# Moving batch 1's first scores, sums and values later in the stream of FFN matmuls

## The chip, the cores and the metric

One core of one Trainium2 chip. The metric is the device time of one execution in microseconds (us); medians of several runs are quoted. Engines: PE is TensorE, DVE is VectorE, ACT is ScalarE, POOL issues the loads, SP issues transposes and stores.

## The reference, cut to what matters

```python
k_proj = einsum('ks,bhsd->bhkd', E, k)            # 8 batches, 8 heads, seq 1024, head_dim 64, 64 projected keys
v_proj = einsum('ks,bhsd->bhkd', F, v)
attn = softmax(q @ k_proj.T / sqrt(64))           # per batch and head
x = (attn @ v_proj) ... reshaped to (8192, 512)
h = maximum(maximum(x @ w1, x @ w2), x @ w3)      # d_ff 768
out = h @ w_out                                   # float32
```

## The kernel before

PE works through 8 batches of two halves ("visits" `(b, ch)`). A visit has 6 FFN steps `up` (12 matmuls of 128x512 each: three weights, four contraction tiles) and 4 output steps `down` (6 matmuls each). The attention of the next batch is cut into small pieces, which a hand-made plan puts behind the steps. Here is the plan of batch 0, and the pieces it names:

```python
def scores(b, g, lo, nsi):        # needs qT and kpT; g is a pair of heads
    t, ns = two()                 # two PSUM banks out of 8
    ... 4 matmuls ...
def sc(b, g, lo=0, nsi=SI):       # scores; its exponential (ACT) is issued "later", in the next step
    ...
def za(b, g, ...):                # sums and values, then ln and exp on ACT, then the scaling on DVE
    z = sums(b, g, lo, nsi)       # needs the exponential
    av = values(b, g, lo, nsi)    # needs the projected values too
    invert(b, g, lo, nsi, z)      # ACT: zl = ln(z); zi = exp(-zl)
    scale_x(b, g, lo, nsi, av)    # DVE: xT = av * zi, which the FFN of batch b reads
def vproj(b): ...                 # 16 matmuls, needs v of batch b in SBUF
def qd(b, parts=1): ...           # DVE copies of q, then a DMA transpose per part -> qT

def up(b, ch, jt):
    ...
    early = jt == 0               # first step of a visit: the last contraction tile at the end,
    for i in range(3):            # so 9 matmuls run before xT of the last pair is needed
        h.append(bank())
        up_mm(h[i][0], i, b, ch, jt, range(NCT - early))
    ...                           # [cut] then h1s copy (ACT), two maxima (DVE)

# plan(0); a key is (half, step), steps 6 to 9 are output steps
(0, 7): [qd(1, 2), za(0, 2, *c1)],
...
(1, 0): [kproj(1)],
(1, 1): [kt(1)],
(1, 2): [sc(1, 0), sc(1, 1), vproj(1), ld(2)],
(1, 3): [za(1, 0), sc(1, 2)],
(1, 4): [za(1, 1), sc(1, 3)],
(1, 5): [za(1, 2)],
(1, 7): [za(1, 3)],
```

The copies of an output step go from PSUM to SBUF on ACT (`down(..., "s")`), except in the very first visit. Banks are dealt by a small clock model in the program, so moving a piece can deal all later banks anew.

The softmax here doesn't subtract the row's maximum and nothing guards it: scores larger than these inputs give would overflow.

Of the kernel before, what the change touches and what calls it, by code (L numbers as in the profile page):

```python
# [15 lines left out]
def kernel(  # L16
# [62 lines left out]
    def bank():  # L79
        n = min(range(8), key=lambda n: free[n])  # L80
        deal((n,))
        return psum_t[:, n, :], (n,)
# [110 lines left out]
    def scores(b, g, lo, nsi):  # L193
        t, ns = two()
        n = nsi // 2
        for c in range(2):
            for hp in range(2):
                rows = slice(hp * HALF, (hp + 1) * HALF)
                at = g * SI + lo + c * n
                nc.tensor.matmul(  # L200
                    out=t[c * HALF:(c + 1) * HALF, hp, 0:n * P],
                    lhsT=kpTs[b][rows, g, :],
                    rhs=qTs[b][rows, at:at + n, :],
                    start=True, stop=True,
                )
        return t[:, :, 0:n * P], ns, pe(n * MM / 4 + 0.1)

    def exps(b, g, lo, nsi, sc):
        t, ns, ready = sc
        pTs[b, g, lo] = att.tile([P, 2, CHUNK], BF16, name="pT", bufs=4)[:, :, 0:nsi * HALF]  # L210
        nc.scalar.activation(out=pTs[b, g, lo], in_=t, func=AF.Exp, scale=scale)  # L211
        runs("s", ready, 0.17 + nsi * 0.107, ns)
# [14 lines left out]
    def sums(b, g, lo, nsi):  # L227
        return pair_mm(b, g, lo, nsi, lambda rows, hp: ones[rows])

    def invert(b, g, lo, nsi, z):  # L230
        t, ns, ready = z
        zl = att.tile([P, 2, CHUNK], FP32, name="zl", bufs=1)[:, :, 0:nsi * HALF]
        nc.scalar.activation(out=zl, in_=t, func=AF.Ln)  # L233
        runs("s", ready, 0.17 + nsi * 0.107, ns)
        if nsi == SI:
            zi = att.tile([P, 2, CHUNK], FP32, name="zi", bufs=2)
        else:
            zi = att.tile([P, 2, CHUNK // 2], FP32, name="zi0", bufs=4)
        nc.scalar.activation(out=zi, in_=zl, func=AF.Exp, scale=-1.0)  # L239
        zis[b, g, lo] = zi, runs("s", ready, 0.17 + nsi * 0.107)  # L240

    def values(b, g, lo, nsi):
        if b not in xTs:
            xTs[b] = att.tile([P, NCT, SI, P], BF16, name="xT")
        return pair_mm(b, g, lo, nsi, lambda rows, hp: vps[b][rows, 2 * g + hp, :])

    def scale_x(b, g, lo, nsi, av):
        t, ns, ready = av
        zi, when = zis.pop((b, g, lo))
        nc.vector.tensor_tensor(  # L250
            out=xTs[b][:, g, lo:lo + nsi, :].rearrange("a (c s) p -> a c (s p)", c=2),
            in0=t, in1=zi, op=ALU.mult,
        )
        runs("v", max(ready, when), 0.17 + nsi * 0.13, ns)
# [8 lines left out]
    def sc(b, g, lo=0, nsi=SI):  # L263
        def f():
            t = scores(b, g, lo, nsi)
            later.append(lambda: exps(b, g, lo, nsi, t))
        return f

    def za(b, g, lo=0, nsi=SI, then=False):
        def f():  # L270
            z = sums(b, g, lo, nsi)
            av = values(b, g, lo, nsi)
            invert(b, g, lo, nsi, z)
            if then:
                later.append(lambda: scale_x(b, g, lo, nsi, av))
            else:
                scale_x(b, g, lo, nsi, av)
        return f
# [84 lines left out]
    def vproj(b):  # L363
        def f():
            t, ns = bank()
            proj(b, 2, t, (LO, HI), 4 * D)

            vps[b] = att.tile([P, H, D], BF16, name="vp")
            for hh, hs in enumerate((LO, HI)):
                i = t[hh * HALF:(hh + 1) * HALF, 0:4 * D].rearrange("a (h d) -> a h d", d=D)  # L370
                for to in range(2):
                    copy("sv"[hh], vps[b][to * HALF:(to + 1) * HALF, hs, :], i, ns, 0.4)
        return f
# [161 lines left out]
                most(hs[:, jt] if i == 1 else hTs[0, 0][:, jt, :], *h[jt], hs[:, jt])  # L535
                then((i, jt))

    def up(b, ch, jt):
        if jt == 0:
            hTs[b, ch] = ffn_sb.tile([P, NJT, CHUNK], BF16, name="hT")  # L540
        h, done = [], []
        early = jt == 0
        for i in range(3):
            h.append(bank())
            up_mm(h[i][0], i, b, ch, jt, range(NCT - early))
            done.append(clock["pe"])
        if early:
            for i in range(3):
                up_mm(h[i][0], i, b, ch, jt, (NCT - 1,))
                done[i] = clock["pe"]  # L550
        h1s = ffn_sb.tile([P, CHUNK], FP32, name="h1s")
        nc.scalar.copy(out=h1s, in_=h[0][0])  # L552
        r = runs("s", done[0], 0.6, h[0][1])
        run_later()
        m12 = ffn_sb.tile([P, CHUNK], FP32, name="m12")
        nc.vector.tensor_tensor(out=m12, in0=h[1][0], in1=h1s, op=ALU.max)  # L556
        runs("v", max(r, done[1]), 0.69, h[1][1])
        most(hTs[b, ch][:, jt, :], *h[2], m12)
# [50 lines left out]
    def ld(b):  # L609
        return lambda: load(b)  # L610

    def plan(b):
        n = b + 1
        if b == 0:
            c1 = (SPC, SPC)
            return {
                (0, 6): [za(0, 1, *c1), sc(0, 3, *c1)],
                (0, 7): [qd(1, 2), za(0, 2, *c1)],
                (0, 8): [za(0, 3, *c1)],
                (1, 0): [kproj(1)],  # L620
                (1, 1): [kt(1)],
                (1, 2): [sc(1, 0), sc(1, 1), vproj(1), ld(2)],
                (1, 3): [za(1, 0), sc(1, 2)],
                (1, 4): [za(1, 1), sc(1, 3)],
                (1, 5): [za(1, 2)],
                (1, 7): [za(1, 3)],
            }
        if b == 1:
            return {
                (0, 1): [qd(2)],  # L630
                (0, 5): [kproj(2), vproj(2), ld(3)],
                (0, 6): [kt(2)],
                (0, 7): [sc(2, 0)],
                (0, 9): [za(2, 0), sc(2, 1)],
                (1, 1): [za(2, 1), sc(2, 2)],
                (1, 3): [za(2, 2), sc(2, 3)],
                (1, 5): [za(2, 3)],
                (1, 6): [qd(3)],
            }
        if b == 2:  # L640
            return {
                (0, 2): [kproj(3), vproj(3), ld(4)],
                (0, 3): [kt(3)],
                (0, 4): [sc(3, 0)],
                (0, 6): [za(3, 0), sc(3, 1)],
                (1, 0): [za(3, 1), sc(3, 2), qd(4)],
                (1, 2): [za(3, 2), sc(3, 3), kproj(4), vproj(4), ld(5)],
                (1, 4): [kt(4)],
                (1, 5): [za(3, 3), sc(4, 0)],
            }  # L650
        if n == B:
            return {}
        out = {
            (0, 1): [za(n, 0), sc(n, 1)],
            (0, 3): [za(n, 1), sc(n, 2)],
            (0, 9): [za(n, 2), sc(n, 3)],
            (1, 3): [za(n, 3)],
        }
        if n + 1 < B:
            out[0, 6] = [qd(n + 1)]  # L660
            out[0, 9] += [kproj(n + 1), vproj(n + 1)]
            out[1, 1] = [kt(n + 1)]
            out[1, 3] += [sc(n + 1, 0)]
        if n + 2 < B:
            out[1, 1] += [ld(n + 2)]
        return out

    for b in range(B):
        p = plan(b)

        def behind(ch, step):
            for f in p.get((ch, step), []):
                f()

        for ch in range(NCHUNK):
            if (b, ch) == (0, 0):
                c1 = (SPC, SPC)
                up_first({
                    (0, 0, 5): [lambda: v_pair(2)],
                    (0, 1, 2): [lambda: x(2)],  # L680
                    (0, 1, 5): [lambda: v_pair(3), ld(1)],
                    (0, 2, 2): [lambda: x(3)],
                    (2, "a", 2): [qp(0, (0, 1), *c1)],
                    (2, "a", 4): [qp(0, (2, 3), *c1)],
                    (2, 0): [sc(0, 0, *c1)],
                    (2, 2): [sc(0, 1, *c1)],
                    (2, 4): [za(0, 0, *c1, then=True), sc(0, 2, *c1)],
                })
                run_later()
                behind(0, NJT - 1)  # L690
            else:
                for step in range(NJT):
                    up(b, ch, step)
                    behind(ch, step)
            for tt in range(SPC):
                down(b, ch, tt, "v" if (b, ch) == (0, 0) else "s")
                behind(ch, NJT + tt)
# [30 lines left out]
```

## Time and profile before

| | |
|---|---|
| time | 406.68 us median of 3 runs (406.23 to 407.16) |
| PE busy | 391.0 of 405.1 us |
| longest PE wait inside the run | 1.80 us, for qT of batch 1 |
| from the first scores (57.41) to the next visit's first h1s copy (78.43) | 21.02 us |

The page of the kernel before, its lines on PE, the granted clock by slice, the DMA engines by slice, and the chain that ended last. The digits are tenths in 40 slices of 10.1 us.

```profile
PE 391.0 (97%) x2330; PEld 178.2 (44%) x2374; DVE 199.9 (49%) x309; ACT 190.9 (47%) x278; POOL 31.6 (8%) x44
...
PEclk9999999999999999999999999999999999999999
DMA  9999999949927994991898119950510202020202
...
PE 83%; DMA 10%; ACT 2%; issue 1%; POOL 1%; DVE 1%; ACTq 0%; POOLq 0%
```

PE is the bound, at full clock. But in the first eight slices (81 us) the DMA engines are busy 90% or more, and the chain gives DMA 10% of the span: up to 57 us the loads of weights and of q lead it.

The timeline of PE where batch 1's attention begins (start us, duration us, engine, line, operation, out<-in, count, and in brackets the idle time just before and what ended it; a trace can lack a few matmul records, so a count of x11 stands for 12). L496 are FFN matmuls, L200 scores, L284 projections, L220 sums and values, L591 output steps:

```profile
52.86 2.75 PE L496 MATMUL banks<-xT,w_sb 128*128 128x512 bf16 x12
57.41 0.63 PE L200 MATMUL banks<-qT,kpT 64*64 64x512 bf16 x8 [1.80 <-DMA qT<-q_p]
57.97 1.06 PE L284 MATMUL banks<-v_t,efT 128*64 128x256 bf16 x16
58.97 2.76 PE L496 MATMUL banks<-xT,w_sb 128*128 128x512 bf16 x11
61.66 0.41 PE L220 MATMUL banks<-pT,ones 64*64 64x512 bf16 x4
```

and the first line of ACT's timeline after 78 us, the next visit's first h1s copy:

```profile
78.43 0.58 ACT L552 COPY h1s<-banks 128x512 f32<-128x512 f32 x1 [1.57 <-PE banks L496]
```

PE ends FFN step 2 at 55.61 (52.86 + 2.75), and stands until 57.41 for the transposed queries. Then scores, value projection, and step 3 follow.

When the two loads came: first the load of v of batch 1, then the transpose of the first half of q. Each fence has the issue and the time from issue to landing:

```profile
L189 POOL DMA_DIRECT2D v_t<-in_v_dram x1: 873/873/873, 25.8 to 25.8; - x1
...
DMA to landing us min/median/max: 30.4/30.4/30.4
```

```profile
L331 SPq DMA_TRANSPOSE qT<-q_p x1: 8108/8108/8108, 44.6 to 44.6; - x1
...
DMA to landing us min/median/max: 12.8/12.8/12.8
```

v landed at 25.8 + 30.4 = 56.2, qT at 44.6 + 12.8 = 57.4. Both are later than PE wants them (55.61).

### The profile page before, as it was taken

To read this page: it belongs to the slowest core of one execution; us is meant where nothing else is said; L and a number is where in the kernel's file an instruction comes from. 1 tells how busy PE (TensorE), PEld (TensorE's weight loads), DVE (VectorE), ACT (ScalarE), POOL (GpSimd) and SP (SyncE) were. 2 spreads that over 40 slices of the span, in tenths; PEclk is the share of its full clock that TensorE was granted. 3 is DMA by queue.
4 is the path that set the end of the run, shared out by engine and by line. 5 is a ranking of instruction groups with operands and counts; after the bars stand their busy time and mean duration, and the time that the engine had idled before them with its cause. 6 is when DMAs were issued, how large, how long until landed. Compare 5 with 4: busy or idle time off the path is not lost.

```text
span 405.1 us, 5869 instructions
## 1 busy us (share of the span) xinstructions
PE 391.0 (97%) x2330; PEld 178.2 (44%) x2374; DVE 199.9 (49%) x309; ACT 190.9 (47%) x278; POOL 31.6 (8%) x44
## 2 busy tenths in 40 slices
PE   6899989999999999999999999999999999999996
PEld 3444433444444535444544445444544444444443
DVE  2348746462655527537353655626464363525251
ACT  2612429624763366555544555437535556432322
POOL 7440011002000100200200002000000000000000
PEclk9999999999999999999999999999999999999999
DMA  9999999949927994991898119950510202020202
GB/s 148 206 205 207 230 200 166 242 114 126 256 34 210 177 237 106 146 246 25 213 187 181 44 37 236 205 148 2 141 69 1 104 2 104 2 104 0 105 0 104
DMA packets 62667, 53.33 MB, mean 132 GB/s; under 512 B 30128, under 2 KB 58288, under 8 KB 62640
## 3 DMA queue, kind: packets, MB, share of 16 engines
q0 software_dynamic: 28512, 28.31, 44.0%
q1 hardware_dynamic: 33984, 24.51, 19.7%
q8 instruction: 18, 0.29, 0.3%
q10 hardware_dynamic: 144, 0.13, 0.1%
q14 instruction: 9, 0.07, 0.1%
HBM read 57.15 MB, written 16.78 MB: 183 GB/s over the span
## 4 chain that ended last, share of the span: by engine, by line
PE 83%; DMA 10%; ACT 2%; issue 1%; POOL 1%; DVE 1%; ACTq 0%; POOLq 0%
PE banks L496 55%; PE banks L591 19%; PE banks L220 4%; DMA q_t<-in_q_dram 3%; DMA qT<-q_p 3%; DMA w_sb<-in_moe_w_dram 3%; PE banks L284 3%; PE banks L200 2%; ACT pT L211 1%; ACT zl L233 1%; DVE xT L250 1%; ACT zi L239 1%; DMA out_dram<-o_sb 0%; POOL k_t L147 0%; POOL q_t L152 0%
## 5 line engine op out<-in xcount | busy, mean ns | idle before, releaser
L496 PE MATMUL banks<-xT,w_sb 128*128 128x512 bf16 x1118 | 254.7, 379 | 2.8 <-issue 0.6
L496 PEld LDWEIGHTS <-w_sb 128*128 128x128 bf16 x1152 | 109.5, 98 | 136.8 <-issue 9.8
L556 DVE TENSOR_TENSOR m<-banks,h1s 128x512 f32<-128x512 f32 x90 | 62.0, 689 | 85.1 <-ACT h1s L552 53.8
L552 ACT COPY h1s<-banks 128x512 f32<-128x512 f32 x90 | 52.4, 582 | 89.9 <-PE banks L496 87.2
L591 PE MATMUL banks<-wout_sb,hT 128*128 128x512 bf16 x370 | 84.8, 379 | 0.7 <-issue 0.3
L250 DVE TENSOR_TENSOR xT<-banks,zi 128x1024 bf16<-128x1024 f32 (+1 forms) x36 | 39.8, 1106 | 75.8 <-ACT zi L239 56.4
L506 DVE TENSOR_TENSOR hT<-banks,m 128x512 bf16<-128x512 f32 x90 | 62.3, 692 | 10.1 <-DVE m L556 0.5
L99 ACT COPY o_sb<-banks 128x512 f32<-128x512 f32 (+1 forms) x60 | 34.8, 580 | 53.0 <-PE banks L591 52.9
L591 PEld LDWEIGHTS <-hT 128*128 128x128 bf16 x378 | 36.0, 98 | 45.4 <-DVE hT L506 2.8
L233 ACT ACTIVATE zl<-banks 128x1024 f32<-128x1024 f32 (+1 forms) x36 | 33.5, 930 | 29.8 <-PE banks L220 28.9
L211 ACT ACTIVATE pT<-banks 128x1024 bf16<-128x1024 f32 (+1 forms) x36 | 33.2, 931 | 14.4 <-PE banks L200 14.4
L239 ACT ACTIVATE zi<-zl 128x1024 f32<-128x1024 f32 (+1 forms) x36 | 34.6, 962 | 1.1
L189 POOL DMA_DIRECT2D q_t<-in_q_dram x7 | 6.1, 878 | 204.1 <-DMA qT<-q_p 141.7
L200 PE MATMUL banks<-qT,kpT 64*64 64x512 bf16 (+1 forms) x144 | 13.7, 358 | 2.2 <-DMA qT<-q_p 1.8
L284 PEld LDWEIGHTS <-efT 128*64 128x64 bf16 x256 | 12.8, 110 | 5.0 <-issue 4.6
L220 PE MATMUL banks<-pT,ones 64*64 64x512 bf16 (+1 forms) x144 | 13.9, 376 | 0.8 <-DVE xT L250 0.3
L220 PE MATMUL banks<-pT,vp 64*64 64x512 bf16 (+1 forms) x144 | 13.3, 356 | 0.1
L99 DVE CAST vp<-banks 64x256 bf16<-64x256 f32 (+1 forms) x18 | 7.1, 396 | 9.3 <-ACT vp L99 5.9
L220 PEld LDWEIGHTS <-ones 64*64 64x64 bf16 x144 | 4.5, 103 | 14.6 <-issue 13.5
L99 ACT CAST vp<-banks 64x256 bf16<-64x256 f32 x14 | 5.1, 364 | 11.1 <-PE banks L284 10.9
L284 PE MATMUL banks<-k_t,efT 128*64 128x256 bf16 (+1 forms) x144 | 8.7, 263 | 1.3 <-DMA k_t<-in_k_dram 1.2
L99 DVE COPY q_p<-q_t 128x1024 bf16<-128x1024 bf16 x28 | 10.0, 420 | 0.0
(46 smaller groups left out, 96.7 us busy)
## 6 DMA issues: line engine op xcount, KB each, us to landing
out_dram<-o_sb SPq DMA_DIRECT2D x30, 512.0 KB, 2.9
q_t<-in_q_dram POOLq DMA_DIRECT2D x7, 1024.0 KB, 9.6
k_t<-in_k_dram POOLq DMA_DIRECT2D x7, 1024.0 KB, 13.8
v_t<-in_v_dram POOLq DMA_DIRECT2D x7, 1024.0 KB, 20.4
w_sb<-in_moe_w_dram POOLq DMA_DIRECT2D x5, 384.0 KB, 12.1
k_t<-in_k_dram POOLq DMA_DIRECT2D x2, 512.0 KB, 9.4
v_t<-in_v_dram POOLq DMA_DIRECT2D x4, 256.0 KB, 12.4
wout_sb<-in_moe_w_out_dram POOLq DMA_DIRECT2D x1, 768.0 KB, 16.3
```

The costliest lines, as they stand in the source:

```text
L99: done = {"v": nc.vector.tensor_copy, "s": nc.scalar.copy, "g": nc.gpsimd.tensor_copy}[eng](out=o, in_=i)
L211: nc.scalar.activation(out=pTs[b, g, lo], in_=t, func=AF.Exp, scale=scale)
L220: nc.tensor.matmul(out=t[hp * HALF:(hp + 1) * HALF, c, 0:nsi * HALF], lhsT=w(rows, hp), rhs=p[rows, hp, :], start=True, stop=True,)
L233: nc.scalar.activation(out=zl, in_=t, func=AF.Ln)
L239: nc.scalar.activation(out=zi, in_=zl, func=AF.Exp, scale=-1.0)
L250: nc.vector.tensor_tensor(out=xTs[b][:, g, lo:lo + nsi, :].rearrange("a (c s) p -> a c (s p)", c=2), in0=t, in1=zi, op=ALU.mult,)
L284: nc.tensor.matmul(out=t[hh * HALF:(hh + 1) * HALF, 0:width], lhsT=efT[:, si, (kv - 1) * KP:kv * KP], rhs=qkv[b][kv][:, heads[hh], si, :], ...
L496: nc.tensor.matmul(out=h, lhsT=w_sb[i][:, ct, jt * P:(jt + 1) * P], rhs=xTs[b][:, ct, ch * SPC:(ch + 1) * SPC, :], start=(ct == first), st ...
L506: nc.vector.tensor_tensor(out=o, in0=h, in1=other, op=ALU.max)
L552: nc.scalar.copy(out=h1s, in_=h[0][0])
L556: nc.vector.tensor_tensor(out=m12, in0=h[1][0], in1=h1s, op=ALU.max)
L591: nc.tensor.matmul(out=o_ps, lhsT=hTs[b, ch][:, jt, tt * P:(tt + 1) * P], rhs=wout_sb[:, jt, :], start=(jt == 0), stop=(jt == NJT - 1),)
```

## The change

Its intent: not to stand for qT. The value projection (which does not need it) goes first, then 8 FFN matmuls of step 3, and only then the scores, in the middle of the step. The sums and values come one place later, so that the exponentials have time; the last ones land in output step 2.

```diff
-    def up(b, ch, jt):
+    def up(b, ch, jt, mid=None):
...
             done.append(clock["pe"])
+            if i == 1 and mid:
+                mid()
...
-                (1, 2): [sc(1, 0), sc(1, 1), vproj(1), ld(2)],
-                (1, 3): [za(1, 0), sc(1, 2)],
-                (1, 4): [za(1, 1), sc(1, 3)],
-                (1, 5): [za(1, 2)],
-                (1, 7): [za(1, 3)],
+                (1, 2): [vproj(1), ld(2)],
+                (1, (3, "mid")): [sc(1, 0), sc(1, 1)],
+                (1, 4): [za(1, 0), sc(1, 2)],
+                (1, 5): [za(1, 1), sc(1, 3)],
+                (1, 7): [za(1, 2)],
+                (1, 8): [za(1, 3)],
...
-                    up(b, ch, step)
+                    up(b, ch, step, lambda: behind(ch, (step, "mid")))
```

## The prediction

> **What bounds the kernel.** TensorE. The page gives PE 391.0 of 405.1 us busy (97%), the chain of waits is 83% PE, granted clock 1.0 throughout. So only PE's pauses can be won (an FFN matmul takes 0.216 us). The largest is in batch 0's second half: PE ends FFN step 2 at 55.61 us and stands 1.80 us for the transposed queries of batch 1 (the waits view: PE scores <- DMA qT, 1.8 us, once; landed 57.37). Small pauses follow (two sums wait for VectorE's scaled values); the next visit's first step ends at 78.8 (its h1s copy starts at 78.43).
>
> **What changes.** Nothing is added or removed, only moved. The first two scores go behind the value projection (0.99 us) and 8 FFN matmuls of step 3 (1.73 us); the four sums-and-values move from ends of steps 3, 4, 5 and output step 1 to ends of steps 4, 5 and output steps 1, 2. The banks are dealt anew.
>
> **Step by step, from trace durations.**
> 1. The value projection now comes first at 55.61, but v of batch 1, issued at 25.82, took 30.4 us to land (DMA view): 56.2. So 0.6 of the 1.8 us stays, as a wait for v. The projection ends at 57.25, 8 matmuls at 59.0; the scores (qT there since 57.37) run unhindered to 59.5; step 3 ends near 60.4, where the old kernel ended it at 61.65. Gain here 1.2 us.
> 2. The dependent chain starts about 1.3 us later relative to PE's work: exp 0.96 us a piece, ln 1.04, exp 1.06, multiply 1.23. The Trainium skill ("TensorE: Matmul & The Clock Gate", engine queue depths) says ScalarE and VectorE are strict FIFO; this trace agrees (an h1s copy of data ready by 63.7 starts at 64.38, as the exp before it ends). My replay: first sums 63.05, first scaled values 66.75; the second sums wait 0.3 us for that bank pair and the fourth scores 0.1 us for a max. ScalarE is then busy without a break from 69.0 to 75.6 (copies 0.48 each, exp, two ln/exp pairs).
> 3. The last sums come at 72.2, their ln waits for ScalarE until 73.45, the scaled values are there at 76.85. PE, through output step 3 and nine early matmuls of the next visit, arrives at 75.95: a new wait of about 0.9 us in front of the last three matmuls (PE FFN <- DVE xT). They end at 77.5, against 78.8 before.
>
> Net: -1.3 us, nearly all critical, since PE runs on without slack after. Loads do not move: their issues on POOL wait for qT's second half (landed 59.1).
>
> **Predicted: 405.3 us**, range 404.2 to 406.5. Faster by over 2%: 0.01; within 2%: 0.98; slower by over 2%: 0.01.
>
> **What would show it.** The 1.8 us PE <- qT wait gone; a PE wait of 0.3 to 0.8 us for v (or the projection starting at 56.2 after a gap); step 3's end near 60.4; a PE wait of 0.5 to 1.3 us on xT near 76 us; everything after shifted by about 1.3 us.
>
> **What would make it wrong.** v landing earlier or later than in this one trace (it decides 0.6 us); ScalarE's backlog smaller, so that step 3's wait vanishes (404.4), or larger, so that the gain is eaten up (406.5); the different deal of banks making new waits in batches 1 and 2.

## The result, and the profile after

| | before | changed | ratio, 95% interval |
|---|---|---|---|
| first job, 4 runs each | 406.52 us | 406.06 us | 0.9985 (0.9961 to 1.0009) |

A ratio is the mean time of one kernel's runs over the mean of the other's in the same rounds, so it is not quite the ratio of the medians in the table. The interval even includes 1. The time lies inside the range on record, 0.8 us above its centre.

The page of the changed kernel, the same four lines:

```profile
PE 392.0 (97%) x2331; PEld 178.8 (44%) x2374; DVE 200.1 (49%) x309; ACT 191.1 (47%) x278; POOL 31.7 (8%) x44
...
PEclk9989999999999999999999999999999999999999
DMA  9999999948927994991898119950510202020202
...
PE 89%; DMA 4%; ACT 2%; issue 2%; POOL 1%; DVE 1%; ACTq 0%; DVEq 0%; POOLq 0%
```

The chain of waits is now 89% PE and 4% DMA: the wait for qT has left it. But the third digit of the granted clock is an 8. The stretches of 2 us from 16 to 24 us (busy time of each engine, then the granted clock, DMA share, GB/s):

```profile
16.00:18.00 2.00, 1.76 (x25) 0.96 (x21) 1.28 (x3) 1.65 (x4) 0.72 (x1) 1.00 1.16 201
18.00:20.00 2.00, 1.03 (x3) 0.39 (x4) 0.30 (x1) 1.60 (x3) 0.79 (x1) 0.80 1.23 205
20.00:22.00 2.00, 2.00 (x11) 1.15 (x10) 0.00 (x0) 0.00 (x0) 0.98 (x3) 0.50 1.17 208
22.00:24.00 2.00, 1.78 (x13) 0.86 (x12) 0.80 (x2) 0.00 (x0) 1.63 (x3) 0.84 1.16 208
```

The clock was granted at 0.80, 0.50 and 0.84, in a part of the program that the change does not touch. That is (0.20 + 0.50 + 0.16) x 2 = 1.7 us of full clock lost. PE came to the end of step 2 at 57.05, not 55.61. That the lost clock made it late is likely, not proven: in a later trace with the same loss (the warmed changed kernel) PE came at 57.1, and in the traces at full clock not later than 56.1. The timeline of PE, same window and columns as before:

```profile
54.30 2.75 PE L496 MATMUL banks<-xT,w_sb 128*128 128x512 bf16 x12
56.98 1.06 PE L284 MATMUL banks<-v_t,efT 128*64 128x256 bf16 x16
57.98 1.90 PE L496 MATMUL banks<-xT,w_sb 128*128 128x512 bf16 x8
59.81 0.63 PE L200 MATMUL banks<-qT,kpT 64*64 64x512 bf16 x8
...
63.93 0.41 PE L220 MATMUL banks<-pT,ones 64*64 64x512 bf16 x4
...
67.81 0.41 PE L220 MATMUL banks<-pT,ones 64*64 64x512 bf16 x4 [0.35 <-DVE xT L250]
...
75.30 2.11 PE L496 MATMUL banks<-xT,w_sb 128*128 128x512 bf16 x9
78.07 2.10 PE L496 MATMUL banks<-xT,w_sb 128*128 128x512 bf16 x8 [0.67 <-DVE xT L250]
```

and the same copy on ACT:

```profile
78.48 0.59 ACT L554 COPY h1s<-banks 128x512 f32<-128x512 f32 x1 [1.25 <-PE banks L496]
```

In this stretch PE waits for no load any more. In their place it waits 0.35 us at the second sums (67.81) and 0.67 us at 78.07, both for DVE's multiply that writes the scaled values (xT): by the program, the sums need the two banks that it reads, and the FFN matmuls the values themselves. The wait at 78.07 stands in front of the last three matmuls of the next visit's first step, as forecast.

This trace invites a wrong sum. From the end of step 2 to the next visit's first h1s copy it shows 78.48 - 57.05 = 21.43 us, against 78.43 - 55.61 = 22.82 before: a gain of 1.39 us. But PE came 1.44 us late here, when v had landed (25.8 + 29.2 = 55.0) and qT too (46.1 + 10.4 = 56.5). The old kernel, coming as late, would not have waited 1.80 us for qT either.

### The profile page after: what moved, and what is told of

Read it like the earlier page. It is cut to its first block, busy times and chain, and to the rows that moved or that the text cites. A ratio compares the mean times of both kernels' runs of the same rounds, so it can differ in the third digit from the quotient of the medians.

```text
span 405.0 us, 5872 instructions
## 1 busy us (share of the span) xinstructions
PE 392.0 (97%) x2331; PEld 178.8 (44%) x2374; DVE 200.1 (49%) x309; ACT 191.1 (47%) x278; POOL 31.7 (8%) x44
## 4 chain that ended last, share of the span: by engine, by line
PE 89%; DMA 4%; ACT 2%; issue 2%; POOL 1%; DVE 1%; ACTq 0%; DVEq 0%; POOLq 0%
PE banks L496 61%; PE banks L593 19%; PE banks L220 4%; PE banks L284 3%; DMA w_sb<-in_moe_w_dram 3%; PE banks L200 2%; DVE xT L250 1%; ACT zl L233 1%; ACT zi L239 1%; DMA out_dram<-o_sb 0%; POOL k_t L147 0%; ACT pT L211 0%; PE banks L425 0%; POOL q_t L152 0%; POOL v_t L147 0%
## 5 line engine op out<-in xcount | busy, mean ns | idle before, releaser
L380 PE MATMUL banks<-warm 128*128 128x512 bf16 x22 | 8.2, 499 | 1.5 <-DVE warm L170 1.2
```

## The experiments

Twelve runs of ten kernels, four to a job, each timed in 5 rounds beside the kernel before. The three jobs ran on three chips, so a time is compared with the others of its own job. All gave correct results. In the tables "stretch" is the time from the start of the value projection (where it is not the first piece, from what is said) to the next visit's first h1s copy. It begins at a landing or at PE's arrival, so it leaves out how early PE or the load came.

### Was the gain hidden by the clock? The change again, and fillers

The first theory (A): the change is worth 1.4 us and the clock hid it. The rival (B): it is worth less. The changed kernel was run again unaltered.

> The changed kernel again, unaltered. Theory A: the change is worth 1.3 to 1.4 us at its place (from the end of FFN step 2 of batch 0's second half to the h1s copy of the next visit's first step: 22.82 us before, 21.43 in the profile after), and the clock, granted at half for about 3.4 us near 20 us in the profiled run, hid most of it in the times. Then runs of granted clock 1.0 should have spans near 403.5, and runs of 0.995 to 0.996 near 405, for both kernels alike about 1.5 us apart; the pooled ratio is -0.1 to -0.35%. Theory B: the 1.4 us is given back later and the kernel is only 0.4 us faster at equal clock. If PE reaches the projection at 55.6, a wait of 0 to 0.6 us for v shows.

Measured: 405.42 us against 406.37, ratio 0.9982 (0.9970 to 0.9994), so 0.7 us. Its trace has a granted clock of 1.0 and a span of 404.3 us, against the 403.5 that theory A wanted (the job's three other runs at clock 1.0 had 403.3 to 403.6, so this span alone refutes nothing), and here PE came early. The timeline of PE:

```profile
53.20 2.75 PE L496 MATMUL banks<-xT,w_sb 128*128 128x512 bf16 x12
56.32 1.06 PE L284 MATMUL banks<-v_t,efT 128*64 128x256 bf16 x16 [0.37 <-DMA v_t<-in_v_dram]
57.32 1.90 PE L496 MATMUL banks<-xT,w_sb 128*128 128x512 bf16 x8
59.15 0.63 PE L200 MATMUL banks<-qT,kpT 64*64 64x512 bf16 x8
59.71 3.63 PE L496 MATMUL banks<-xT,w_sb 128*128 128x512 bf16 x16
63.26 0.41 PE L220 MATMUL banks<-pT,ones 64*64 64x512 bf16 x4
...
74.63 2.11 PE L496 MATMUL banks<-xT,w_sb 128*128 128x512 bf16 x9
77.40 2.97 PE L496 MATMUL banks<-xT,w_sb 128*128 128x512 bf16 x13 [0.66 <-DVE xT L250]
```

PE stands 0.37 us for v (landed 56.3), the forecast's step 1. qT landed at 57.4, before the scores. The next visit's first h1s copy starts at 77.81, only 0.62 us ahead of the old kernel's 78.43, though the loads landed within 0.1 us of the same times. So theory A's 1.3 to 1.4 us are not there. Nothing is given back later either (B's form of it): from that copy to the end are 326.5 us, before 326.6.

Over all jobs, runs of the changed kernel with a granted clock of 0.996 or less had spans of 404.5 us on average (3 runs), those of 0.999 or more 403.7 (11 runs). For the kernel before it was 404.8 (4 runs) against 404.5 (23 runs). At full clock the two differ by 0.8 us, not by 1.4, so theory A falls: its 403.5 for the changed kernel was nearly right, but the kernel before runs 0.6 us under the 405.1 of its profiled run. The averages also suggest that the old kernel, which stood for qT anyway, lost less to a slow clock early on; three and four runs don't settle it.

In the first trace of the changed kernel PE stood 1.16 us for the first FFN weights (17.81 to 18.97) just before the clock fell. So four more warming matmuls were put into that wait, in the changed kernel and in the old one:

```diff
-    def idle(n):
+    def idle(n, more=0):
...
-        for _ in range(n):
+        for _ in range(n + more):
...
     x(1)
-    idle(1)
+    idle(1, 4)
     at(17.4)
```

> The changed kernel with four more warming matmuls (0.86 us) in the wait for the first FFN weights at 17.8 to 19.0 us. Theory A: [...]the clock stays at 1.0 in every run, the spread of the times shrinks, and the median falls to 404.5 to 405.2; if the weights land before the fillers end it costs up to 0.35 us. Rival: the clock falls as often as before, and the time is that of the changed kernel plus 0 to 0.4 us.

> The kernel before with the same four warming matmuls. With the clock at 1.0 in both, the difference between this and the warmed changed kernel is the worth of the change: theory A 1.0 to 1.6 us, theory B 0.3 to 0.6 us.

Measured: the warmed changed kernel 405.99 us (0.9989, 0.9976 to 1.0001), the warmed old one 405.98 us (0.9997, 0.9984 to 1.0009). The clock still fell: 4 of the 5 warmed changed runs had a mean of less than 0.999. In the profiled one it fell at 12 to 16 us, ahead of the fillers, after PE had stood 1.86 us for k (9.03 to 10.89). So the fillers failed at their purpose, and the pair cannot serve as a measurement at equal clock: the expected 0.3 to 1.6 us between the two did not show at all in the medians. Their traces are of use all the same. The old kernel's stretch from its scores to the copy is 56.29 to 77.31 = 21.02 us, as before; the changed one's from the projection is 57.01 to 78.51 = 21.50.

### What the gain consists of

By now the traces agree on two numbers:

| kernel | stretch begins with | stretch, us |
|---|---|---|
| before; warmed before | scores, at qT's landing | 21.02; 21.02 |
| changed, four traces (two of them with PE late) | projection, at v's landing or PE's arrival | 21.50; 21.49; 21.50; 21.50 |

v lands 1.2 to 1.3 us ahead of qT in the three traces of kernels that still stand for qT (before 56.2 and 57.4; warmed 55.0 and 56.3; the control below 55.3 and 56.6). New theory, called the landing theory: the change swaps a wait for qT for a wait for v, which wins that 1.2 to 1.3 us, and its longer chain costs 21.50 - 21.02 = 0.48 us. The difference, 0.7 to 0.8 us, is an estimate from traces; the three jobs' ratios times 406.4 give 0.6, 0.7 and 0.9.

### Where the 0.48 us come from: ACT's queue

```diff
-                down(b, ch, tt, "v" if (b, ch) == (0, 0) else "s")
+                down(b, ch, tt, "v" if b == 0 else "s")
```

> The changed kernel with the four output copies of batch 0's second half on VectorE in place of ScalarE. If the new wait of 0.67 us before the next visit's last three matmuls of its first step comes from ScalarE's backlog (three copies of about 0.48 us lie between the sums' logarithms and exponentials), the last scaled values come 0.8 to 1.4 us earlier, the wait goes, and the stretch from the end of step 2 to the next visit's first h1s copy falls from 21.43 to 20.7 to 20.9 us. Rival: the chain is set by the place of the last sums alone, the wait stays above 0.4 us, or VectorE's longer queue (copy 0.69 before the multiply 1.23) puts it back.

Measured: 404.76 us against 406.37, ratio 0.9963 (0.9952 to 0.9975), and 0.66 us under the changed kernel's median of the same job (405.42). The wait fell from 0.66 to 0.16 us and the stretch from 21.50 to 20.96 us. The last scaled values came 0.56 us earlier (FFN matmuls at 76.84, not 77.40), less than the 0.8 expected, so a little of the wait stays. About 0.2 us of the gain is not the wait's: from the copy to the end this trace takes 326.3 us, the changed kernel's 326.5. The timeline of ACT in the repeated changed kernel:

```profile
71.00 0.59 ACT L99 COPY o_sb<-banks 128x512 f32<-128x512 f32 x1
71.47 1.05 ACT L233 ACTIVATE zl<-banks 128x1024 f32<-128x1024 f32 x1
72.55 1.06 ACT L239 ACTIVATE zi<-zl 128x1024 f32<-128x1024 f32 x1
73.51 0.57 ACT L99 COPY o_sb<-banks 128x512 f32<-128x512 f32 x1
73.98 1.03 ACT L233 ACTIVATE zl<-banks 128x1024 f32<-128x1024 f32 x1
75.03 1.06 ACT L239 ACTIVATE zi<-zl 128x1024 f32<-128x1024 f32 x1
...
77.81 0.58 ACT L554 COPY h1s<-banks 128x512 f32<-128x512 f32 x1 [1.25 <-PE banks L496]
```

and in the kernel with the copies on DVE:

```profile
72.32 1.06 ACT L239 ACTIVATE zi<-zl 128x1024 f32<-128x1024 f32 x1
73.41 1.02 ACT L233 ACTIVATE zl<-banks 128x1024 f32<-128x1024 f32 x1
74.47 1.06 ACT L239 ACTIVATE zi<-zl 128x1024 f32<-128x1024 f32 x1
77.25 0.58 ACT L554 COPY h1s<-banks 128x512 f32<-128x512 f32 x1 [1.72 <-PE banks L496]
```

and, in the same kernel, the line of PE with the wait that is left:

```profile
76.84 5.34 PE L496 MATMUL banks<-xT,w_sb 128*128 128x512 bf16 x24 [0.16 <-DVE xT L250]
```

In the changed kernel, the last logarithm (73.98) waits for the copy at 73.51, which waits for the exponential at 72.55, while its sums are there since 73.2; with the copies on DVE, logarithm and exponential follow without copies. The Trainium skill ("ScalarE: Activation LUTs", What ACT_TABLE_LOAD costs) gives 186 ns + 0.833 ns per element, from which I estimate 1039 ns for 1024 elements, and an overlap of about 93 ns; these traces show 1.02 to 1.06 us and 0.96 us from the exponential to the copy behind it, so they agree.

The control, the same edit on the kernel before:

> Control: the kernel before with only the output copies of batch 0's second half on VectorE. If the wait on ScalarE's chain before the next visit's last matmuls was made by the change (later sums between the copies), this does nothing here, because the old kernel's last scaled values were there 1.1 us before use: 406.2 to 406.6, within 0.2 us of before. Rival: the copies hold the chain up in the old kernel too, and it gains 0.4 us or more.

Measured: 406.34 us against 406.42, ratio 1.0001 (0.9989 to 1.0014). Moving the copies gains the old kernel nothing in time. Its trace is not quite neutral: a new wait of 0.22 us for xT stands before the last values, the stretch is 21.43 us (56.64 to 78.07) in place of 21.02, and from the copy to the end are 326.3 us in place of 326.5 or 326.6. But with the copies on ACT or on DVE, the old kernel has no wait for xT before the next visit's last three matmuls, and neither has the kernel of the next section, with the sums at their old places. So it is the later place of the sums, among the output copies, that made the wait.

### Which part of the change carries the gain?

The scores moved, the sums left at their old places (from the changed kernel):

```diff
-                (1, 4): [za(1, 0), sc(1, 2)],
-                (1, 5): [za(1, 1), sc(1, 3)],
-                (1, 7): [za(1, 2)],
-                (1, 8): [za(1, 3)],
+                (1, 3): [za(1, 0), sc(1, 2)],
+                (1, 4): [za(1, 1), sc(1, 3)],
+                (1, 5): [za(1, 2)],
+                (1, 7): [za(1, 3)],
```

> Part of the change alone: the value projection and the first two scores moved as in the change, the sums and values left at their old places (ends of steps 3, 4, 5 and of output step 1). Landing theory (the gain is which landing PE stands for, qT at 57.4 or v at 56.2, less 0.45 us that the moved chain costs): the first sums, at the end of step 3, come only four matmuls (0.9 us) after the scores and must wait for the exponential, about 0.5 to 1 us; the stretch from the projection to the next visit's first h1s copy is 21.0 to 21.6 us against 21.48 in the changed kernel; time within 0.4 us of the changed kernel's (405.4). Rival (the later sums are what gains): the time goes back to 406.4 or worse.

Measured: 405.22 us against 406.44, ratio 0.9977 (0.9964 to 0.9991), stretch 56.53 to 77.72 = 21.19 us. The expected wait of 0.5 to 1 us for the exponential at the first sums did not show: they started at 60.90, right after the step's matmuls. The cost fell where the kernel before has it too: the third scores took 0.80 us (before 0.81, in the changed kernel 0.39), PE waited 0.23 and 0.39 us for xT at the next two sums (before 0.17 and 0.18), and no longer at the end.

The projection in front of the scores, nothing else (from the kernel before):

```diff
-                (1, 2): [sc(1, 0), sc(1, 1), vproj(1), ld(2)],
+                (1, 2): [vproj(1), sc(1, 0), sc(1, 1), ld(2)],
```

> The smallest form: the kernel before with the value projection put in front of the two scores at the end of step 2, nothing else moved. Landing theory: PE stands 0.4 to 0.6 us for v, projects to 57.3, and meets qT as it lands (57.3 to 57.5, a wait of 0 to 0.2 us), so the projection's 1.0 us is hidden in what was the wait: time 405.2 to 405.7, as good as the whole change. Rival (the eight matmuls and the later sums are needed): 406.0 or more.

Measured: 405.08 us against 406.44, ratio 0.9973 (0.9961 to 0.9986). The expected wait for v did not show: in this run v landed at 55.51, as PE came, and the scores waited 0.21 us for qT. Since it stood in another job than the whole change, both were run once more on one chip:

> The changed kernel a third time, beside the swap on one chip. Landing theory: 0.5 to 1.0 us faster than before (405.4 to 405.9); its stretch from the projection to the next visit's first h1s copy 21.4 to 21.5 us again. Rival: what the earlier jobs showed was the chips' difference, and it equals the swap.

> The swap alone again (projection in front of the two scores, nothing else). Landing theory: it holds all that the change is worth and does not pay the 0.3 us of the later sums: 0.2 to 0.5 us faster than the changed kernel on the same chip (405.0 to 405.3), stretch 21.0 to 21.3 us. Rival: equal to the changed kernel within 0.1 us, so the eight matmuls and later sums cost nothing.

Measured: change 405.31 us, ratio 0.9977 (0.9964 to 0.9989); swap 405.38 us, ratio 0.9976 (0.9962 to 0.9989); before 406.42. The swap is as fast as the whole change. I had expected it to be faster by 0.2 to 0.5 us; the medians fit the rival. The timeline of PE in the swap's second trace:

```profile
52.80 2.75 PE L496 MATMUL banks<-xT,w_sb 128*128 128x512 bf16 x12
55.61 1.06 PE L284 MATMUL banks<-v_t,efT 128*64 128x256 bf16 x16
56.83 0.63 PE L200 MATMUL banks<-qT,kpT 64*64 64x512 bf16 x8 [0.15 <-DMA qT<-q_p]
57.39 2.76 PE L496 MATMUL banks<-xT,w_sb 128*128 128x512 bf16 x11
```

The projection fills the time until qT comes, and 0.15 us of wait is left. The stretches are 21.24 us (swap) and 21.50 us (change): the swap has the shorter chain. In these two runs the difference did not come out in the medians; the runs of each spread over 0.7 to 1.1 us, as wide as the effect itself, so a difference of 0.2 us can't be ruled out.

### Both waits gone

The changed kernel with the projection too behind the eight matmuls, and that with the copies on DVE as well:

```diff
-                (1, 2): [vproj(1), ld(2)],
-                (1, (3, "mid")): [sc(1, 0), sc(1, 1)],
+                (1, (3, "mid")): [vproj(1), sc(1, 0), sc(1, 1), ld(2)],
```

> The changed kernel with the value projection too put behind the eight matmuls of step 3, just in front of the scores. PE reaches it at 57.4, after v (56.3) and about when qT lands, so neither wait is left. Landing theory: 0.4 to 0.7 us faster than the changed kernel (404.7 to 405.0) in runs where PE came early, the wait on xT near 77 us still there at 0.4 to 0.9 us. Rival (ScalarE's backlog alone sets the end): the end of the stretch does not move, 405.4, and the wait on xT grows by the 0.5 us won.

> Both mends together: the projection behind the eight matmuls, and the output copies of batch 0's second half on VectorE. If the two costs are separate (0.4 to 0.6 us of wait for v; 0.53 us of wait on ScalarE's chain), they add: 404.0 to 404.4 us, the best of all. If they are one and the same slack, it is no better than the kernel with the copies moved alone (404.76).

Measured, both in the job of the swap's first run (before 406.44): 404.75 us, ratio 0.9969 (0.9957 to 0.9982), and 404.59 us, ratio 0.9966 (0.9952 to 0.9980). In the first, no wait on a load is left and the wait on xT is still 0.67 us, as expected. In the second that wait is 0.16 us, but the time falls by only 0.16 us where 0.5 was expected, so it is nearer to the rival's 404.76 than to the 404.0 to 404.4 of two separate costs. The traces show both: the stretch is 0.53 us shorter (19.17 us, from 58.27 to 77.44, against 19.70, from 57.55 to 77.25), but from the h1s copy to the end the second takes 326.5 us and the first 326.3. Many of the later banks are dealt otherwise; that this is why is not shown. Whether that holds in the runs whose traces I did not read stays open.

Last, the projection and both scores behind the first four matmuls of step 3, the sums at their old places (from the kernel before):

```diff
-    def up(b, ch, jt):
+    def up(b, ch, jt, mid=None):
...
+            if i == 0 and mid:
+                mid()
...
-                (1, 2): [sc(1, 0), sc(1, 1), vproj(1), ld(2)],
+                (1, (3, "mid")): [vproj(1), sc(1, 0), sc(1, 1), ld(2)],
...
-                    up(b, ch, step)
+                    up(b, ch, step, lambda: behind(ch, (step, "mid")))
```

> The kernel before with projection and both scores behind the first four matmuls of step 3, sums and values at their old places. PE reaches the projection 0.9 us later than in the swap, after v (56.3 at the latest), and the scores after qT; the exponentials start no later than where the swap stands for v. Landing theory: no wait on a load, stretch no longer than the swap's, 0.1 to 0.5 us faster than the swap (404.6 to 405.0). Rival: the exponentials start later, the sums wait for it, and nothing is won over the swap.

Measured: 404.95 us against 406.42, ratio 0.9963 (0.9950 to 0.9975); the changed kernel on the same chip had 405.31. The timeline of PE:

```profile
52.49 3.62 PE L496 MATMUL banks<-xT,w_sb 128*128 128x512 bf16 x16
56.03 1.06 PE L284 MATMUL banks<-v_t,efT 128*64 128x256 bf16 x16
57.03 0.63 PE L200 MATMUL banks<-qT,kpT 64*64 64x512 bf16 x8
57.81 1.67 PE L496 MATMUL banks<-xT,w_sb 128*128 128x512 bf16 x7 [0.16 <-issue]
59.47 0.49 PE L220 MATMUL banks<-pT,ones 64*64 64x512 bf16 x4
```

Four matmuls (0.87 us) cover the end of both loads: v landed at 55.2 and qT at 56.5, the projection runs at 56.03 and the scores at 57.03, without a wait. The sums, at their old places, cause no wait at the end. By the ratios this version is about 1.5 us faster than before, the change 0.9 us in the same job. It beats both kernels in the medians, though its interval and the change's overlap. The version with the copies on DVE has the same ratio in another job.

One count puts most of these times in order: from qT's landing to the copy (landings to the hundredth from the trace), in the kernels that still stand for a load, in traces with PE early.

| kernel | qT's landing to copy, us | gain by the traces, us | gain by the ratios, us |
|---|---|---|---|
| before; warmed before | 21.06; 21.06 | | |
| changed, two traces | 20.37; 20.32 | 0.7 | 0.6, 0.7 and 0.9 |
| swap, two traces | 20.06; 20.06 | 1.0 | 1.1 and 1.0 |
| scores moved, sums not | 20.01 | 1.0 | 0.9 |
| changed, copies on DVE | 19.85 | 1.2, and 0.2 after the copy | 1.5 |
| before, copies on DVE (control) | 21.47 | -0.4, and 0.2 to 0.4 after the copy | 0.0 |

In the traces, then, the swap is better than the change by 0.3 us, which is what the later sums cost. In the times of five runs that is too small to see.

## Why the prediction was right, and where its sizes were off

1. **"The 1.8 us PE <- qT wait gone; a PE wait of 0.3 to 0.8 us for v": right.** The wait for qT is in no trace of the change. With PE early, the wait for v is 0.37 and 0.40 us in two traces; with PE late (clock), it is absent. "v landing earlier or later than in this one trace" was named as the risk. It moved between 55.0 and 56.5 over the traces, and qT moved with it; what counts is the 1.2 to 1.5 us between them.
2. **"Step 3 ends near 60.4": 60.7** in the repeated run (the last maximum of step 3 starts at 60.78), where v landed at nearly the time of the forecast. So the gain at that place was 0.9 us, not 1.2. Each change from one kind of matmul to another took about 0.1 us more than the counts times 0.216 us: the eight matmuls 1.83 us, not 1.73; the next sixteen 3.55, not 3.46.
3. **"The second sums wait 0.3 us": 0.35. "A new wait of about 0.9 us" on xT: 0.66 to 0.68**, inside the 0.5 to 1.3; ACT's backlog is its cause, shown by the copies moved to DVE and by the control.
4. **"They end at 77.5, against 78.8 before": about 78.2** (two more matmuls after the first of the three, whose copy starts at 77.81). PE came to the wait at 76.7, not 75.95. The last sums came at 72.8, not 72.2, and xT at 77.36, not 76.85. After the wait the first matmul took from 77.40 to about 77.8 to its end, not 0.216 us. The Trainium skill ("TensorE: Matmul & The Clock Gate", Single matmul latency) gives (398 + N)/2.4 ns for one warm matmul, which makes an estimate of 379 ns for N = 512, and the mean of one FFN matmul on the kernel's profile page is 379 ns too; I had costed it as one in a row. So the term mis-sized was the length of the moved chain, by about 0.5 us over the handovers, and the matmul after the stop, by 0.16 us. Of the forecast 1.3 us, 0.62 us remained in that trace.
5. **"Net: -1.3 us": -0.6, -0.7 and -0.9 us** in three jobs, with intervals from 1.6 us faster to 0.4 us slower in the first of them, and clear of zero in the other two. "PE runs on without slack after" held: the time from the h1s copy to the end did not move (326.6 and 326.5 us), so the new deal of the banks, named as a risk, cost nothing there. Two of the three medians, 405.42 and 405.31 us, lie on the predicted 405.3 in part by luck: the gain was smaller than forecast, but the kernel before ran at 406.4 us, not at the 406.68 of the first table. And the range reached up to 406.5, nearly to no gain at all, so the range says little; the waits that were forecast are the test.
6. **What the prediction did not see:** a simple swap would do as well as the whole change. The eight matmuls and the later sums solve a problem (scores before qT, sums before the exponential) that the projection's 1.0 us nearly solves alone, and the later sums bring one of their own.

## What to carry to other kernels

When an engine stands for a load, ask which load it will stand for next: a reorder that leads from one load to the next wins only the time between the two landings, not the whole wait; work that needs neither, like the four matmuls of the last version, can cover both. Measure such a change from the landing, not from the engine's arrival, since an engine that comes late for another reason (here, it seems, a clock drop) makes the old wait vanish as well. And moving a piece to a later place puts its dependants behind whatever that place issues on an in-order engine; look at that engine's queue there before moving.

## What the Trainium skill lacked or had wrong

- "TensorE: Matmul & The Clock Gate" (Part 1: The HAM clock gate) gives half clock as the state after an idle window of about 3.4 us. The traces agree with the size (0.80, 0.50 and 0.84 over 6 us make 3.4 us at half), but no idle time of that length came before it: in the changed kernel's trace PE stood 1.16 us (17.81 to 18.97) and was busy 1.76 and 1.03 of 2 us from 16 to 20 us; in the warmed one it stood 1.86 us (9.03 to 10.89) and the clock fell at 12 to 16 us. The kernel before stood 1.23 us (9.10 to 10.33) and kept the full clock. What share of busy time is enough is not given.
- "DMA: Bandwidth & Descriptors" (Latency and other measured facts) gives an effective 261 GB/s for one kernel's DMA transposes, and says nothing of what loads in flight do to them. Here the first half of q (0.5 MB) took 10.4 to 12.9 us from issue to landing beside the loads (DMA moved 213 GB/s in all from 44 to 56 us in the last version's trace); the whole of the next batch's q (1 MB) took 7.1 us at 83.6 us, with few loads about. That loads in flight are the reason was not tested.
- "TensorE: Matmul & The Clock Gate" (Back-to-back issue gap) gives about 131 ns per matmul as the sustained spacing for N = 512. Here twelve FFN matmuls in a row, each with its weight load, took 2.59 us, so 216 ns each, which is the value that the section gives for an isolated gap.
- No page gives a time for going from one kind of matmul to another (other shape, other tile position); "TensorEngine Tiling (Array Packing)" (Key Properties) says that a change of tiling mode drains the engine, but not how long that takes. Here eight FFN matmuls between a projection and scores took 0.1 us more than eight times 216 ns.
